# Delta-rule attention and an MLP on one core: w's product on two quarters of the array, copied out in one piece

## The chip, the cores and the metric

One core of a Trainium2 chip. The metric is the device time of one launch in microseconds (us). Engines: PE is TensorE (PEld its weight loads), ACT is ScalarE, DVE is VectorE, POOL is GpSimd, SP is SyncE, which issues most DMAs.

## The reference

For 4 batches and 8 heads, 768 steps and 48 dimensions a head, all float32, a state of 48x48 is carried along the steps by a delta rule; the attention's output, 3072 rows of 384, goes through an MLP with a squared ReLU.

```python
k_n = k / (np.linalg.norm(k, axis=-1, keepdims=True) + 1e-06)
for t in range(S):
    kt, vt, bt = (k_n[:, :, t], v[:, :, t], beta[:, :, t, None])
    y[:, :, t] = np.einsum('bhd,bhde->bhe', q[:, :, t], state)
    v_old = np.einsum('bhde,bhd->bhe', state, kt)
    state = state + bt[:, :, :, None] * np.einsum('bhd,bhe->bhde', kt, vt - v_old)
...
h = np.maximum(x @ w_in, 0.0)
return (h * h @ w_out).astype(np.float32)
```

## The kernel before, in words

**Units.** The 768 steps are cut into 12 units of 64 (C = 64). Inside a unit the recurrence is written as products of small matrices, so that a unit needs the state only at its start. For each unit and each of the 32 pairs of batch and head there is a 64x64 triangular matrix; its inverse, transposed and scaled, lies in `tt` (t in `state_part`). The unit's product w = t' v', where v' is v less what the state already holds for the keys (vt), gives the corrected values. From w come the state's update (keys' rows `kp` times w) and the unit's output y (masked query products `ap` times w, on top of queries times state). The MLP runs on a unit's 256 rows while the next unit's recurrence goes on.

**Layout.** 128 partitions are two halves of 64 (`half_rows(0)`, `half_rows(1)`). The index x (8 values) counts pairs of batch and heads, b (2) is a batch's place, j (2) a head's place and also picks one of two PSUM banks. The rows of a head (b, j) of t, vt, kp, ap and w lie in half b ^ j. A matmul of TensorE with 64 rows and 64 columns of weights takes one quarter of the array: the half of the partitions that it reads and the half of the PSUM partitions that it writes.

**The products of a unit**, all in `state_part` (line 720 on), 64 matmuls each (x by b by j):
- line 734: keys' rows times queries and state, two groups of four x; vt is corrected by VectorE (line 736), the query part is copied to `ap` by ScalarE (737) and masked by GpSimd.
- line 746: queries times state, into gy.
- line 752: w's product. In unit 0 (`first`) head (b, j) is read from half b ^ j and written to half b ^ j; in all other units it is read from half b ^ j and written to half b. So unit 0 uses two quarters, same half to same half, and the others all four.
- lines 759 to 764: ScalarE copies w from PSUM to SBUF. In unit 0 that is one copy (760). In the others the head j = 0 is in its place already (762), and for j = 1 each half of PSUM goes to the other half of SBUF (764, two copies of 64 partitions).
- line 774: the state's update, read from half b ^ j, written to the partitions of dims(j), four quarters, in all units but the last; VectorE adds it to the state (777).
- line 791: y's second part, read from half b ^ j, written to half b; ScalarE copies y (794).

Line 658 is unit 0's query products; it uses four quarters.

**Order.** The engines' queues keep the order in which the program is written. `weave` mixes the recurrence's generators with pieces of the MLP (`moe`: lines 845 and 829 are its matmuls, 852 to 855 ScalarE's squared ReLU and rounding, 820 VectorE's remainder, 805 to 808 the transposes of y and their split into x_h and x_l) by tables of fractions, A["odd"], A["even"] and A[u]. After w's product the queue of TensorE has MLP matmuls, then line 774. VectorE also works on the inverse of the next pair of units (lines 531 and 533) in small steps.

Of the kernel before, what the change touches and what calls it, by code (L numbers as in the profile page):

```python
# [20 lines left out]
def kernel(  # L21
# [89 lines left out]
    nc = tc.nc  # L111
# [23 lines left out]
    def g_tile():  # L135
        return ps_g.tile([P, 2, bank], F32, name="g")
# [56 lines left out]
    def need(*keys):  # L193
        assert all(key in done for key in keys), keys
# [126 lines left out]
    def half_rows(b):  # L321
        return slice(b * C, (b + 1) * C)

    def dims(j):
        return slice(j * C, j * C + D)
# [5 lines left out]
    def load_rows(dst, src, u):  # L331
        t = slice(u * C, (u + 1) * C)
        for b in range(2):
            for j in range(2):
                nc.sync.dma_start(out=dst[half_rows(b ^ j), j],
                                  in_=by_j(src)[j, 2 * b:2 * b + 2, :, t].rearrange("b p t d -> t (b p) d"))
# [307 lines left out]
    def masked(u):  # L644
        for b in range(2):
            half = ap[0][half_rows(b)].rearrange("p j x t -> p (j x) t")
            nc.gpsimd.affine_select(out=half, in_=half, pattern=[[0, 2 * X], [1, C]], base=0, channel_multiplier=-1,  # L647
                                    compare_op=ALU.is_gt, fill=0.0)
        done.add(("ap", u))
# [29 lines left out]
    def wide(g):  # L679
        return g[:, :, :XD].rearrange("p j (x e) -> p j x e", x=X)  # L680
# [4 lines left out]
    def turned_y(w, g):  # L685
        w_ = w.rearrange("p j x d -> p (j x d)")
        xt = g[:, :, :KT * 2 * C].rearrange("p b (k n t) -> p b k n t", k=KT, n=2)
        begun = set()

        def heads(j, p):  # L690
            for n in range(2):
                for part in range(2):
                    strip = 3 * p + part + j
                    kt, rows_ = strip // 4, slice(strip % 4 * HB, (strip % 4 + 1) * HB)
                    for r in range(2):
                        b = r ^ j
                        c0 = (j * X + n * NP + p) * C + (part * HB if j == 0 else part * HB - QB)
                        nc.tensor.matmul(xt[rows_, b, kt, n], lhsT=w_[half_rows(r), c0:c0 + HB],
                                         rhs=ap[0][half_rows(r), j, n * NP + p],
                                         start=(b, strip % 4) not in begun, stop=True, skip_group_check=True)  # L700
                        begun.add((b, strip % 4))
                yield

        for j in range(2):
            for ps in ((0, 2), (1, 3)):
                both = [heads(j, p) for p in ps]
                for n in range(2):
                    for gen in both:
                        next(gen)
            if j == 0:  # L710
                nc.tensor.drain()
        x_h, x_l = xs[0] = [mpool.tile([P, KT, 2 * P], F32R, name=name, bufs=1) for name in ("x_h", "x_l")]
        for k0, k1 in ((0, 1), (1, KT)):
            for b in range(2):
                cols = [x[:, k0:k1].rearrange("p k (n b t) -> p b (k n) t", n=2, b=2)[:, b] for x in (x_h, x_l)]
                src = xt[:, b, k0:k1].rearrange("p k n t -> p (k n) t")
                nc.scalar.copy(out=cols[0], in_=src)
                nc.vector.tensor_tensor(out=cols[1], in0=src, in1=cols[0].bitcast(F32), op=ALU.subtract)

    def state_part(u):  # L720
        first, last = u == 0, u == units - 1
        vt, t = vts[u], tt[:, :, u % 2].rearrange("p j x c t -> p j x (c t)")
        s = state.rearrange("p (b x) e -> p b x e", b=2)
        need(("v", u), ("keys", u), *[("y", u - 1)][:u])
        if not first:
            need(("queries", u))
            ap[0] = apool.tile([P, 2, X, C], F32, name="ap")
            for x0 in range(0, X, 4):
                ps = g_tile()[:, :, :4 * (C + D)].rearrange("p j (x n) -> p j x n", x=4)
                for x in range(4):  # L730
                    for b in range(2):
                        for j in range(2):
                            n = b * X + x0 + x
                            nc.tensor.matmul(ps[half_rows(b ^ j), j, x], lhsT=kts[u][dims(j), n], rhs=qs[dims(j), n],  # L734
                                             start=True, stop=True)
                nc.vector.tensor_tensor(out=vt[:, :, x0:x0 + 4], in0=vt[:, :, x0:x0 + 4], in1=ps[:, :, :, C:], op=ALU.subtract)  # L736
                nc.scalar.copy(out=ap[0][:, :, x0:x0 + 4], in_=ps[:, :, :, :C])  # L737
            masked(u)
            yield
        need(("queries", u), ("below", u))  # L740
        gy = g_tile() if first else wide(g_tile())
        if not first:
            for x in range(X):
                for b in range(2):
                    for j in range(2):
                        nc.tensor.matmul(gy[half_rows(b), j, x], lhsT=qts[u][dims(j), b * X + x], rhs=s[dims(j), b, x],  # L746
                                         start=x == 0, stop=False, skip_group_check=True)
        ps = wide(g_tile())
        for x in range(X):
            for b in range(2):  # L750
                for j in range(2):
                    nc.tensor.matmul(ps[half_rows(b ^ j if first else b), j, x], lhsT=t[half_rows(b ^ j), j, x],  # L752
                                     rhs=vt[half_rows(b ^ j), j, x],
                                     start=True, stop=True)
        if first:
            w = w0[0][:, :, :, :D]
        else:
            w = apool.tile([P, 2, X, D], F32, name="w")
        if first:
            nc.scalar.copy(out=w, in_=ps)  # L760
        else:
            nc.scalar.copy(out=w[:, 0], in_=ps[:, 0])
            for b in range(2):
                nc.scalar.copy(out=w[half_rows(1 - b), 1], in_=ps[half_rows(b), 1])
        done.add(("w", u))
        yield
        need(("ap", u), ("rows", u))
        def update():
            if not last:
                ps = wide(g_tile())  # L770
                for x in range(X):
                    for b in range(2):
                        for j in range(2):
                            nc.tensor.matmul(ps[dims(j), b, x], lhsT=kp[half_rows(b ^ j), j, x], rhs=w[half_rows(b ^ j), j, x],  # L774
                                             start=True, stop=True)
                for j in range(2):
                    nc.vector.tensor_tensor(out=s[dims(j)], in0=s[dims(j)], in1=ps[dims(j)], op=ALU.add)  # L777

        if first:
            turned_y(w0[0], gy)  # L780
            yield
            update()
            load_rows(kp, k, 1)
            done.update({("y", u), ("x", u)})
            yield
            return
        update()
        for x in range(X):
            for b in range(2):
                for j in range(2):  # L790
                    nc.tensor.matmul(gy[half_rows(b), j, x], lhsT=ap[0][half_rows(b ^ j), j, x], rhs=w[half_rows(b ^ j), j, x],  # L791
                                     start=False, stop=True, skip_group_check=True)
        ys[u] = y = apool.tile([P, 2, H * D], F32, name="y")
        nc.scalar.copy(out=y.rearrange("p n (q j e) -> p j (n q) e", j=2, e=D), in_=gy)  # L794
        done.add(("y", u))
        yield
# [167 lines left out]
    with tc.manual_schedule(engines=engines):  # L964
# [36 lines left out]
        def zeros():  # L1001
            need(("keys", 2), ("queries", 0))
            for b in range(2):
# [8 lines left out]
        chain = dict(A=kk[0], B=kk[1], P=prepare(pair0), I=inverse, G=query_products(0), V=scale_v(0, pair0),  # L1012
                     e=ended(pair0), c=corrected(pair0, 0), d=corrected(pair0, 1), b=below(pair0, 0), a=below(pair0, 1),
                     s=state_part(0))
        once = {"0": lambda: turned_keys(0, kb), "1": lambda: turned_keys(1, kb1), "2": lambda: turned_keys(2, kb3),
                "x": lambda: turned_queries(0, kb2), "y": lambda: turned_queries(1, kb), "l": later_loads,
# [81 lines left out]
```

## Time and profile before

| | us |
|---|---|
| median of 3 runs | 597.77 (596.33 to 599.57) |
| profiled execution, its own time | 595.15 |
| its span, first to last instruction | 593.4 |
| TensorE busy | 557.2 (94%) |
| VectorE busy | 395.2 (67%) |
| ScalarE busy | 334.4 (56%) |
| GpSimd busy | 53.9 (9%) |

The profiled execution is one more run, 2.6 us below the median of the others. A busy share is an average over stages; TensorE's is lower in the first 100 us (set-up, unit 0 and the splitting of the MLP's weights) than after. Weight loads and matmuls overlap, and so do matmuls among themselves, so a burst's busy time is the time from its first start to its last end less its gaps.

### The profile page before, as it was taken

To read this page: it belongs to the slowest core of one execution; us is meant where nothing else is said; L and a number is where in the kernel's file an instruction comes from. 1 tells how busy PE (TensorE), PEld (TensorE's weight loads), DVE (VectorE), ACT (ScalarE), POOL (GpSimd) and SP (SyncE) were. 2 spreads that over 40 slices of the span, in tenths; PEclk is the share of its full clock that TensorE was granted. 3 is DMA by queue.
4 is the path that set the end of the run, shared out by engine and by line. 5 is a ranking of instruction groups with operands and counts; after the bars stand their busy time and mean duration, and the time that the engine had idled before them with its cause. 6 is when DMAs were issued, how large, how long until landed. Compare 5 with 4: busy or idle time off the path is not lost.

```text
span 593.4 us, 21658 instructions
## 1 busy us (share of the span) xinstructions
PE 557.2 (94%) x9728; PEld 532.9 (90%) x9728; DVE 395.2 (67%) x725; ACT 334.4 (56%) x550; POOL 53.9 (9%) x64
## 2 busy tenths in 40 slices
PE   5276899989999999999999999999999999999997
PEld 5256799989899999999999999999999999999997
DVE  2899789899339798359798359797459795430210
ACT  4885578544756454665455566446565346564543
POOL 4020001101002002003002003002003002001000
PEclk9675689999999999999999999999999999999999
DMA  8967630140262050262050361140460330200101
GB/s 244 277 177 287 158 45 2 31 79 1 39 106 25 8 101 1 38 105 27 17 93 2 48 103 16 35 76 3 66 99 3 57 53 4 49 8 1 29 1 27
DMA packets 146668, 37.67 MB, mean 63 GB/s; under 512 B 140272, under 2 KB 143344, under 8 KB 146576
## 3 DMA queue, kind: packets, MB, share of 16 engines
q1 hardware_dynamic: 146496, 36.20, 29.9%
q8 instruction: 76, 1.25, 0.9%
q14 instruction: 16, 0.13, 0.1%
q10 hardware_dynamic: 80, 0.10, 0.0%
HBM read 31.56 MB, written 4.72 MB: 61 GB/s over the span
## 4 chain that ended last, share of the span: by engine, by line
PE 83%; ACT 7%; DVE 5%; DMA 2%; issue 1%; POOL 1%; SPq 1%; POOLq 0%; ACTq 0%
PE h L845 34%; PE o L829 30%; PE g L734 3%; PE g L829 2%; PE g L746 2%; PE g L791 2%; PE g L752 2%; PE g L774 1%; PE g L430 1%; PE g L392 1%; PE h L805 1%; ACT w L246 1%; DMA w<-in_moe_w_out_dram 1%; ACT w L248 1%; DVE w L278 1%
## 5 line engine op out<-in xcount | busy, mean ns | idle before, releaser
L829 PE MATMUL o<-w,h_h 128*128 128x384 f32 x704 | 185.7, 344 | 0.7 <-issue 0.7
L845 PE MATMUL h<-x_h,w 128*128 128x256 f32 x1152 | 173.4, 287 | 1.5 <-DVE x_l L808 1.5
L845 PEld LDWEIGHTS h<-x_h,w 128*128 128x128 f32 x1152 | 156.2, 193 | 4.9 <-issue 2.3
L820 DVE TENSOR_TENSOR h_l<-r,h_h 128x512 fp32r<-128x512 f32 x96 | 66.1, 692 | 125.3 <-ACT h_h L855 125.2
L829 PEld LDWEIGHTS o<-w,h_h 128*128 128x128 f32 x704 | 121.1, 189 | 3.9 <-issue 1.0
L829 PE MATMUL o<-w,h_l 128*128 128x384 f32 x352 | 118.2, 336 | 0.4 <-DVE h_l L820 0.4
L852 ACT ACTIVATE r<-h 128x512 f32<-128x512 f32 x96 | 57.5, 599 | 98.3 <-PE h L845 85.9
L845 PE MATMUL h<-x_l,w 128*128 128x256 f32 x576 | 101.1, 285 | 0.0
L845 PEld LDWEIGHTS h<-x_l,w 128*128 128x128 f32 x576 | 83.5, 193 | 0.0
L829 PEld LDWEIGHTS o<-w,h_l 128*128 128x128 f32 x352 | 66.0, 188 | 0.7 <-DVE h_l L820 0.7
L853 ACT ACTIVATE r<-r 128x512 f32<-128x512 f32 x96 | 60.7, 632 | 3.1
L855 ACT CAST h_h<-r 128x512 fp32r<-128x512 f32 x96 | 59.6, 621 | 3.0
L531 DVE TENSOR_TENSOR tmp<-lt,z 128x31 f32<-128x31 f32 (+15 forms) x155 | 56.4, 364 | 3.7
L533 DVE TENSOR_TENSOR z<-z,tmp 128x31 f32<-128x31 f32 (+15 forms) x155 | 53.1, 343 | 5.3
L647 POOL TENSOR_SCALAR_AFFINE_SELECT ap<-ap 64x1024 f32<-64x1024 f32 x24 | 33.0, 1376 | 245.0 <-ACT ap L737 241.5
L737 ACT COPY ap<-g 128x512 f32<-128x512 f32 x22 | 11.8, 590 | 35.3 <-DVE vt L736 35.3
L777 DVE TENSOR_TENSOR qs<-qs,g 48x768 f32<-48x768 f32 x22 | 20.9, 950 | 14.8 <-PE g L774 14.7
L794 ACT COPY y<-g 128x768 f32<-128x768 f32 x11 | 8.8, 801 | 27.8 <-PE g L791 27.7
L477 POOL MEMSET z<- 128x1024 f32 x5 | 4.8, 955 | 211.9 <-DVE lt L471 211.9
L807 ACT CAST x_h<-h 128x384 fp32r<-128x384 f32 x22 | 10.6, 481 | 23.2 <-PE h L805 23.2
L734 PE MATMUL g<-qs,kt 48*64 48x112 f32 x704 | 19.5, 259 | 0.2 <-DVE mt L449 0.2
L734 PEld LDWEIGHTS g<-qs,kt 48*64 48x64 f32 x704 | 17.1, 133 | 2.0 <-ACT mt L445 0.5
(165 smaller groups left out, 691.3 us busy)
## 6 DMA issues: line engine op xcount, KB each, us to landing
w<-in_moe_w_out_dram SPq DMA_DIRECT2D x8, 768.0 KB, 5.3
w<-in_moe_w_in_dram SPq DMA_DIRECT2D x6, 768.0 KB, 6.9
vt<-in_v_dram SPq DMA_DIRECT2D x48, 96.0 KB, 3.0
kp<-in_k_dram SPq DMA_DIRECT2D x48, 96.0 KB, 2.9
out_dram<-rest SPq DMA_DIRECT2D x47, 96.0 KB, 2.4
kb<-in_q_dram SPq DMA_DIRECT2D x40, 64.0 KB, 2.6
kb<-in_k_dram SPq DMA_DIRECT2D x32, 64.0 KB, 2.8
w<-in_moe_w_in_dram SPq DMA_DIRECT2D x3, 512.0 KB, 6.2
```

Of the source, the lines that this page charges most:

```text
L531: nc.vector.tensor_tensor(out=tmp, op=ALU.mult, in0=lt[:, s:s + 1, s + 1:].broadcast_to([P, nj, nt]), in1=z[:, :nj, s:s + 1].broadcast_to( ...
L533: nc.vector.tensor_tensor(out=z[:, :nj, s + 1:], in0=z[:, :nj, s + 1:], in1=tmp, op=ALU.subtract)
L647: nc.gpsimd.affine_select(out=half, in_=half, pattern=[[0, 2 * X], [1, C]], base=0, channel_multiplier=-1, compare_op=ALU.is_gt, fill=0.0)
L734: nc.tensor.matmul(ps[half_rows(b ^ j), j, x], lhsT=kts[u][dims(j), n], rhs=qs[dims(j), n], start=True, stop=True)
L746: nc.tensor.matmul(gy[half_rows(b), j, x], lhsT=qts[u][dims(j), b * X + x], rhs=s[dims(j), b, x], start=x == 0, stop=False, skip_group_che ...
L777: nc.vector.tensor_tensor(out=s[dims(j)], in0=s[dims(j)], in1=ps[dims(j)], op=ALU.add)
L820: nc.vector.tensor_tensor(out=h_l, in0=r, in1=h_h.bitcast(F32), op=ALU.subtract)
L829: nc.tensor.matmul(o[i], lhsT=a[:, e, i * P:(i + 1) * P], rhs=w_[w], start=(ft == 0 and n == 0), stop=(ft == FT - 1 and n == 2))
L845: nc.tensor.matmul(hp[:, e], lhsT=half_of(("wi", kt, part))[w][:, f], rhs=x[:, kt], start=(n == 0), stop=(n == 3 * KT - 1))
L852: nc.scalar.activation(out=r, in_=hp, func=AF.Relu)
L853: nc.scalar.activation(out=r, in_=r, func=AF.Square)
L855: nc.scalar.copy(out=h_h, in_=r)
```

## The change

In line 752 the output half becomes b ^ j in every unit, as it was in unit 0 alone, so that w lies in PSUM as it is wanted in SBUF; and ScalarE's copies become one copy of 128 partitions in every unit.

```diff
@@ -749,19 +749,14 @@
         for x in range(X):
             for b in range(2):
                 for j in range(2):
-                    nc.tensor.matmul(ps[half_rows(b ^ j if first else b), j, x], lhsT=t[half_rows(b ^ j), j, x],
+                    nc.tensor.matmul(ps[half_rows(b ^ j), j, x], lhsT=t[half_rows(b ^ j), j, x],
                                      rhs=vt[half_rows(b ^ j), j, x],
                                      start=True, stop=True)
         if first:
             w = w0[0][:, :, :, :D]
         else:
             w = apool.tile([P, 2, X, D], F32, name="w")
-        if first:
-            nc.scalar.copy(out=w, in_=ps)
-        else:
-            nc.scalar.copy(out=w[:, 0], in_=ps[:, 0])
-            for b in range(2):
-                nc.scalar.copy(out=w[half_rows(1 - b), 1], in_=ps[half_rows(b), 1])
+        nc.scalar.copy(out=w, in_=ps)
         done.add(("w", u))
         yield
         need(("ap", u), ("rows", u))
```

No other instruction is added, removed or moved on any engine. On ScalarE around w's copy of unit 1 (r and h_h are the MLP's, g a PSUM tile) the order before is:

```order
L852 ACTIVATE r<-h 128x512
L853 ACTIVATE r<-r 128x512
L855 CAST h_h<-r 128x512
L762 COPY w<-g 128x384
L764 COPY w<-g 64x384 x2
L852 ACTIVATE r<-h 128x512
```

and with the change, whose lines from 760 on have numbers smaller by 5:

```order
L847 ACTIVATE r<-h 128x512
L848 ACTIVATE r<-r 128x512
L850 CAST h_h<-r 128x512
L759 COPY w<-g 128x768
L847 ACTIVATE r<-h 128x512
```

The one copy stands where the three stood, in all of units 1 to 11.

## Rows read from the trace of the kernel before

**Rows 1.** The page, parts 1 and 2: busy time; granted clock in 40 slices, in tenths.

```profile
PE 557.2 (94%) x9728; PEld 532.9 (90%) x9728; DVE 395.2 (67%) x725; ACT 334.4 (56%) x550; POOL 53.9 (9%) x64
...
PEclk9675689999999999999999999999999999999999
```

**Rows 2.** The page, part 4: the chain that ended last, by engine.

```profile
PE 83%; ACT 7%; DVE 5%; DMA 2%; issue 1%; POOL 1%; SPq 1%; POOLq 0%; ACTq 0%
```

**Rows 3.** Stretches: from:to, length, each engine's busy time, granted clock, DMA.

```profile
194.00:545.00 351.00, 350.90 (x6086) 338.20 (x6085) 237.82 (x449) 190.79 (x316) 30.05 (x23) 1.00 0.26 43
...
150.00:194.00 44.00, 43.30 (x813) 41.53 (x813) 24.50 (x36) 27.27 (x45) 4.95 (x4) 1.00 0.36 56
```

**Rows 4.** TensorE's waits from 100 to 593 us: total, times, longest.

```profile
PE h L845 <- DVE x_l L808: 1.5, 1, 1.5
PE o L829 <- issue: 0.7, 1, 0.7
PE g L774 <- ACT w L764: 0.6, 1, 0.6
```

**Rows 5.** ScalarE's copies by line: shortest, median, longest in ns; first and last start.

```profile
L762 ACT COPY w<-g x11: 472/480/482, 110.8 to 544.2; 128x384 f32<-128x384 f32 x11
...
L764 ACT COPY w<-g x22: 471/474/478, 111.3 to 545.2; 64x384 f32<-64x384 f32 x22
...
L760 ACT COPY lt<-g x1: 799/799/799, 56.6 to 56.6; 128x768 f32<-128x768 f32 x1
```

**Rows 6.** Timeline of unit 8, TensorE and ScalarE: start, us, what.

```profile
420.65 0.48 ACT L762 COPY w<-g 128x384 f32<-128x384 f32 x1 [0.30 <-PE g L752]
421.15 0.96 ACT L764 COPY w<-g 64x384 f32<-64x384 f32 x2
...
422.83 0.94 PE L774 MATMUL g<-w,kp 64*48 64x48 f32 x64
```

**Rows 7.** w's products: matmuls and loads alone in stretches; durations in units 0, 1.

```profile
52.25:56.60 4.35, 4.03 (x64) 3.77 (x64) 0.50 1.03 413
...
53.30:55.86 2.56, 2.56 (x54) 2.56 (x52) 0.50 1.04 418
...
L752 PE MATMUL g<-vt,tt x60: 303/303/337, 52.3 to 55.9; 64*64 64x48 f32 x60
...
108.20:109.50 1.30, 1.11 (x64) 1.03 (x64) 1.00 0.06 13
...
108.50:109.10 0.60, 0.60 (x56) 0.60 (x49) 1.00 0.00 0
...
L752 PE MATMUL g<-vt,tt x64: 218/218/218, 108.3 to 109.2; 64*64 64x48 f32 x64
```

**Rows 8.** The same of line 658 (unit 0) and line 774 (units 0 and 7).

```profile
34.00:34.90 0.90, 0.90 (x47) 0.90 (x42) 0.50 0.44 132
...
L658 PE MATMUL g<-qs,kt x64: 311/311/366, 33.4 to 35.1; 48*64 48x64 f32 x64
...
60.35:61.11 0.76, 0.76 (x51) 0.76 (x47) 0.50 1.05 416
...
379.32:379.80 0.48, 0.48 (x60) 0.48 (x53) 1.00 0.00 0
...
L774 PE MATMUL g<-w,kp x640: 205/205/240, 112.3 to 510.4; 64*48 64x48 f32 x160
...
L774 PE MATMUL g<-lt,kp x64: 277/277/310, 60.0 to 61.3; 64*48 64x48 f32 x64
```

**Rows 9.** Timeline of unit 1: PE, PEld, ACT and DVE; idle time before in brackets.

```profile
110.85 0.47 ACT L762 COPY w<-g 128x384 f32<-128x384 f32 x1
...
112.34 0.81 PEld L774 LDWEIGHTS g<-w,kp 64*48 64x48 f32 x64 [0.83 <-ACT w L764]
...
122.17 1.02 DVE L808 TENSOR_TENSOR x_l<-h,x_h 128x384 fp32r<-128x384 f32 x2
...
122.87 0.95 PE L845 MATMUL h<-x_h,w 128*128 128x256 f32 x6 [1.48 <-DVE x_l L808]
```

## The prediction

> **What bounds the kernel now.** I read the page first. TensorE is busy for 94% of the span and its clock is granted at nine tenths or more from the seventh slice on [rows 1]; the reader is to see there that the lower digits end with the first sixth of the run, so that almost all units run at full clock. The chain that ended last is 83% TensorE, 7% ScalarE and 5% VectorE [rows 2]. A share over the whole span hides stages, so the third view is the table of stretches: from 194 to 545 us TensorE is busy 350.90 of 351.00 us, from 150 to 194 us 43.30 of 44.00, both at a granted clock of 1.00 [rows 3]. The bursts of w's products of units 3 to 11 lie in the long stretch, that of unit 2 in the one before, that of unit 1 at 108 us, a few us into the clock's last rise. In the long stretch nothing can be hidden beside TensorE: what its queue gains in work, the end gains in time. The fourth view, TensorE's waits after 100 us, confirms it: three entries, 2.8 us in all, and two of them belong to unit 1 (1.5 us for VectorE's x_l, 0.6 us for ScalarE's w); the third waits for no engine [rows 4].
>
> **What the change takes away.** In 11 units (1 to 11) three ScalarE copies of w, 480 ns and twice 474 ns, become one of 128x768. The same form is in the trace: unit 0's copy of w, which already goes in one piece, takes 799 ns [rows 5]. So 1.43 us becomes 0.80 us, 0.63 us a unit and 6.9 us of ScalarE over the run. On the path this is worth nothing in units 2 to 11: TensorE never waits for w there [rows 4]. Unit 8 shows how near it comes: the copies end at 421.15 + 0.96 = 422.11, and TensorE comes to the state's update, their reader, at 422.83 after MLP matmuls that it has anyway [rows 6]. The relief is credited at nothing in these units, since its cover is work that TensorE must do in any case.
>
> **What it adds.** The 64 matmuls of w's product (64x64 weights, 48 columns moving) in a unit are as many as before, in the same place of TensorE's queue. Before, they went over four quarters of the array: each half of the partitions read, into each half of PSUM. Now a half goes to the same half alone: two quarters. The question is what 64 such matmuls take on two quarters. The trace has it: unit 0 already runs this pattern, in the same form, but its stretch was granted 0.50 of the clock (the 1.2 GHz level), while the units after run at 1.00 (2.4 GHz) [rows 7]. So I take the rate at half clock and carry it over by bursts that ran at both.
>
> A window's count holds every matmul that runs in it, so N of them started within the window and one duration more. Unit 0, two quarters, half clock: 54 in 2.56 + 0.303 us, 53.0 ns each, 106 ns for two. Unit 1, four quarters, full clock: 56 in 0.60 + 0.218, 14.6 ns each, 58.4 ns for four [rows 7]. Two other bursts on four quarters bridge the two [rows 8]: the queries' products of unit 0 at half clock, 47 in 0.90 + 0.311, 25.8 ns each, 103 ns for four; and the state's update at both, in unit 0 51 in 0.76 + 0.277 (20.3 ns) and in unit 7 60 in 0.48 + 0.205 (11.4 ns). Two things follow. First, at half clock two matmuls on two quarters take as long (106 ns) as four on four (103 ns): each quarter takes its own next matmul after a time of its own, and half the quarters give half the rate. Second, full clock shortens that time by 20.3 / 11.4 = 1.78.
>
> So at full clock I expect two matmuls every 58.4 ns: 32 pairs instead of 16 fours, 16 x 58.4 = 0.93 us more for each unit (the burst busy 2.04 us instead of 1.11 [rows 7]). The ends: exactly half of 106 ns, 53.0 ns a pair, gives 32 x 53.0 - 16 x 58.4 = 0.76 us; 106 / 1.78 = 59.6 ns a pair gives 0.97 us; and unit 0's whole burst, 4.03 us (more than 64 x 53.0 ns and a duration, 3.7, so it also holds some stall), over 1.78 is 2.26 us, 1.15 us more than 1.11. I choose 0.93 because the same form at full clock is the nearest row.
>
> **Which units pay.** Units 2 to 11: TensorE is full around them, so all ten pay, 9.3 us. Unit 1 is special [rows 9]. There ScalarE is late: TensorE runs out of filler and waits 0.83 us (weights) until w is copied at 112.29. With the change the copy still starts at about 110.85, behind the cast that ends then, and ends at 111.65, while TensorE comes 0.93 us later: this wait goes and the update starts about 0.1 to 0.25 us later. Then TensorE waits again, 1.48 us, at 122.87 for x_l of the next MLP half, which VectorE begins at 122.17 without having waited for it (the row has no idle time before it): its own earlier work set that moment, and a delay of 0.25 us on TensorE vanishes in the 1.48. So unit 1 costs nothing, and also keeps nothing of the shorter copy. If that cover were gone it would pay its 0.93 - 0.83 = 0.1 us, at worst the whole 0.93.
>
> Nothing else goes late: w's copy starts 0.93 us later and ends 0.93 - 0.63 = 0.30 us later, but its reader also comes 0.93 us later, so the slack of 0.72 us in unit 8 (422.11 to 422.83) grows to 1.35. SyncE and GpSimd get nothing new. **Sum:** 10 x 0.93 = +9.3 us, no credit. Against the profiled execution (595.15 us, of which 593.4 span) that is 604.5 us. The three runs shown have a median of 597.77 (596.33 to 599.57); carried to it, 607.1 us, and that is what I forecast, +1.6%.
>
> **A rule that would give another sum.** The Trainium skill ("TensorE: Matmul & The Clock Gate", Part 3, The mechanism) says that a weight load runs beside matmuls in flight only where its row group differs. The order of the row halves (0, 1, 1, 0) is the same before and after; only the column half changes. By that rule alone the burst would last as long as now and the sum would be 0, which is rival (a) below. The trace disagrees with that reading: the state's update of unit 0 has the same order of row halves on four quarters and takes 20.3 ns a matmul at half clock, where unit 0's two quarters take 53.0 [rows 7, 8]; even with 64 weight columns for its 48 that would be 27.
>
> **The rivals.** *(a) The burst is no longer, and nothing is slower.* The place is the rate at full clock: if the order of the row halves sets it, which does not change, and what holds unit 0's burst back is the half clock or the traffic around it, 64 matmuls take 1.11 us again; the point at which this decides is a pair every 29 ns. Then nothing is added, unit 1 loses a wait of 0.83 us that the x_l wait takes back, and the time is 597.8, no change, 0.8 us less at most. For it: no burst on two quarters at full clock is in the trace. Against it: at half clock, the fours of unit 0 ran at twice the rate or more, the state's update beside the same DMA share (1.05 against 1.04) [rows 7, 8]. Chance 0.05. *(b) The clock falls in the burst.* Unit 0 shows the price of a stretch at 0.50: 4.03 us for the burst, 2.92 more than 1.11, over 10 units +29 us, 627 us. Against it: the clock is 1.00 from 150 to 545 us [rows 3], which holds ten units' bursts of small products, and the MLP's full-size matmuls stand on both sides. Chance 0.02. *(c) The burst is longer, but half of it finds a gap*, a time of about 602 or less. It needs idle time on TensorE, of which 0.10 us is left in 351 [rows 3]. Chance 0.03. That the change does not do what it says is hardly open: the order of instructions shows one copy of w a unit, and the quarter follows from the partitions. The forecast keeps 0.90.
>
> **How the numbers follow.** The bounds are 10 x 0.76 = 7.6 us and 11 x 1.15 = 12.7 us over 597.77, 605.4 to 610.5; the runs shown lie 1.4 below and 1.8 above their median, and the profiled execution 2.6 below it. I widen to 602.5 to 611.0. (b) and most of (a) lie outside. About 0.5% (3 us) is what a measurement of this kernel can tell from no change; the forecast, (b) and half of (c) are slower by more, (a) and the rest of (c) the same: slower 0.93, same 0.06, faster 0.01.
>
> **What would show it.** In the profile after: the burst of w's products busy about 2.04 us at full clock (1.9 to 2.3) in each of units 1 to 11, about 29 ns a matmul; one 128x768 copy of w of 0.80 us; no wait of TensorE for w in unit 1, with the x_l wait there shorter by a quarter of a microsecond or less; the update of the state in units 2 to 11 after the same filler; TensorE's busy time in the long stretch still whole. I am wrong if the burst keeps 1.1 us, if a stretch after 150 us has a granted clock below 1.00, or if TensorE gains idle time.

## The result and the profile after

The changed kernel takes 603.38 us (median of 4 runs, 601.18 to 605.48) against 597.05 us for the kernel before in the same comparison: ratio 1.0127, 95% interval 1.0096 to 1.0157, which is 5.7 to 9.4 us more. It is slower, as forecast; the forecast time was 607.1. Compared again with more runs of the kernel before (first experiment below) the ratio was 1.0165 (1.0124 to 1.0206).

One correction to the words ahead of the prediction: x by b by j is 32 products, not 64. The trace shows each of these float32 products as two matmuls and two weight loads; the 64 are what the trace counts, and all rates are for these.

The page of the changed kernel, parts 1, 2 and 4, whose lines answer to [rows 1, 2]; its line numbers from 760 on are smaller by 5 (the state's update is line 769, the MLP's 840 and 824):

```profile
span 600.9 us, 21634 instructions
...
PE 561.7 (93%) x9728; PEld 538.4 (90%) x9728; DVE 395.5 (66%) x725; ACT 327.3 (54%) x528; POOL 53.9 (9%) x64
...
PEclk9675899999999999999999999999999999999999
...
PE 87%; ACT 4%; DVE 4%; DMA 2%; issue 2%; SPq 1%; DVEq 0%; ACTq 0%
```

ScalarE is busy 7.1 us less, where 11 x 0.63 = 6.9 was said, and TensorE 4.5 us more; that is only half of the 9.3 forecast because TensorE was busy 5.3 us less in the set-up, of which more below (the fifth and sixth slices show a higher clock than before). The chain is TensorE's even more than it was.

Stretches of the changed kernel (columns as in [rows 3]):

```profile
150.00:194.00 44.00, 43.50 (x811) 41.99 (x810) 24.38 (x37) 25.38 (x41) 5.13 (x4) 1.00 0.34 54
194.00:552.00 358.00, 357.92 (x6077) 345.40 (x6077) 237.45 (x447) 185.34 (x299) 29.87 (x22) 1.00 0.25 42
```

TensorE is as full as before, and the clock is whole. w's products in units 1 and 7, of line 752 alone, which answer to [rows 7], and ScalarE's copies, which answer to [rows 5]:

```profile
106.90:109.30 2.40, 2.05 (x64) 1.96 (x64) 1.00 0.03 7
...
374.20:376.60 2.40, 2.05 (x64) 1.96 (x64) 1.00 0.00 0
...
L752 PE MATMUL g<-vt,tt x64: 218/218/218, 107.0 to 108.8; 64*64 64x48 f32 x64
...
L759 ACT COPY w<-g x11: 795/802/804, 109.6 to 551.7; 128x768 f32<-128x768 f32 x11
```

The burst is busy 2.05 us instead of 1.11 at full clock; one matmul still lasts 218 ns. Only fewer run at once. (What the 58.4 ns between two matmuls on one quarter consist of, no run here takes apart.) The copy takes 802 ns.

Timeline of unit 8 of the changed kernel, which answers to [rows 6]:

```profile
423.28 2.07 PE L752 MATMUL g<-vt,tt 64*64 64x48 f32 x64
...
425.40 0.80 ACT L759 COPY w<-g 128x768 f32<-128x768 f32 x1 [1.32 <-PE g L752]
...
427.56 0.81 PEld L769 LDWEIGHTS g<-w,kp 64*48 64x48 f32 x64 [0.25 <-issue]
```

w is there at 426.20, 1.36 us before its reader. And unit 1, which answers to [rows 9]:

```profile
109.06 0.62 ACT L850 CAST h_h<-r 128x512 fp32r<-128x512 f32 x1
109.59 0.80 ACT L759 COPY w<-g 128x768 f32<-128x768 f32 x1
...
111.30 0.81 PEld L769 LDWEIGHTS g<-w,kp 64*48 64x48 f32 x64
...
120.92 1.02 DVE L803 TENSOR_TENSOR x_l<-h,x_h 128x384 fp32r<-128x384 f32 x2
...
121.62 0.95 PE L840 MATMUL h<-x_h,w 128*128 128x256 f32 x6 [1.28 <-DVE x_l L803]
```

No wait for w is left; the wait for x_l is 1.28 us instead of 1.48.

Where the time came in is seen by one and the same instruction in both traces: the start of the state's update (line 774 before, 769 after), read from the two timelines, with some starts of line 734 between (differences of unrounded times).

```
                     before    after   after less before
line 734, unit 1      96.81    95.55   -1.27
update, unit 1       112.35   111.30   -1.04
line 734, unit 2     140.07   138.82   -1.25
update, unit 2       159.77   160.13   +0.36
line 734, unit 3     184.81   184.17   -0.64
update, unit 3       204.75   205.04   +0.30
update, unit 4       248.78   249.73   +0.95
update, unit 5       291.91   293.80   +1.88
update, unit 6       335.97   338.76   +2.80
update, unit 7       379.10   382.83   +3.73
update, unit 8       422.83   427.56   +4.73
update, unit 9       465.97   471.63   +5.66
update, unit 10      509.67   516.27   +6.60
line 791, unit 11    550.59   558.11   +7.53
```

Units 2 to 11 together add 8.8 us (from -1.25 to +7.53). From unit 5 on every unit adds 0.91 to 1.00 us, unit 3 adds 0.93 and unit 4 0.65; unit 1 adds 0.02. Unit 2 adds 1.6 and then takes 1.0 back, mostly since each trace has a pause of TensorE there that the other has not, before (first line) and after:

```profile
163.24 0.19 PEld L829 LDWEIGHTS o<-w,h_h 128*128 128x128 f32 x1 [1.02 <-issue]
...
155.12 0.73 PEld L746 LDWEIGHTS g<-qs 48*64 48x64 f32 x43 [0.57 <-issue]
```

Ahead of unit 1 the profiled execution of the changed kernel was 1.27 us faster. The change touches nothing there; what the trace shows to differ is the granted clock, though that it makes up all of the 1.27 us is not shown. The stretch up to line 734, the one from there to the end, and the one from 61.5 to 78.6 us, before:

```profile
0.00:96.81 96.81, 67.26 (x1660) 59.85 (x1661) 77.00 (x130) 67.58 (x107) 11.78 (x32) 0.75 0.66 182
...
96.81:593.40 496.59, 489.91 (x8068) 473.02 (x8068) 318.24 (x596) 266.85 (x444) 42.17 (x32) 1.00 0.24 40
...
61.50:78.60 17.10, 14.28 (x420) 13.19 (x417) 14.00 (x22) 8.70 (x15) 0.00 (x0) 0.60 0.55 102
```

and after:

```profile
0.00:95.55 95.55, 61.98 (x1661) 55.06 (x1661) 77.03 (x130) 67.37 (x107) 11.78 (x32) 0.80 0.66 185
...
95.55:600.90 505.35, 499.75 (x8068) 483.34 (x8068) 318.47 (x596) 259.92 (x422) 42.15 (x32) 1.00 0.24 40
...
61.50:78.60 17.10, 12.40 (x505) 11.02 (x497) 14.86 (x24) 9.37 (x16) 0.00 (x0) 0.90 0.55 108
```

In the set-up the same work (1660 and 1661 matmuls) ran at a granted clock of 0.75 on average in one and 0.80 in the other; between 61.5 and 78.6 us it was 0.60 and 0.90. TensorE was busy 5.3 us less there, and 9.8 us more from line 734 on, for the same 8068 matmuls: 4.5 in all.

### The profile page after: what moved, and what is told of

Its sections match the earlier page's. It is cut to its first block, busy times and chain, and to the rows that moved or that the text cites. A ratio compares the mean times of both kernels' runs of the same rounds, so it can differ in the third digit from the quotient of the medians.

```text
span 600.9 us, 21634 instructions
## 1 busy us (share of the span) xinstructions
PE 561.7 (93%) x9728; PEld 538.4 (90%) x9728; DVE 395.5 (66%) x725; ACT 327.3 (54%) x528; POOL 53.9 (9%) x64
## 3 DMA queue, kind: packets, MB, share of 16 engines
q8 instruction: 76, 1.25, 0.8%
## 4 chain that ended last, share of the span: by engine, by line
PE 87%; ACT 4%; DVE 4%; DMA 2%; issue 2%; SPq 1%; DVEq 0%; ACTq 0%
PE h L840 34%; PE o L824 30%; PE g L752 3%; PE g L734 3%; PE g L824 2%; PE g L746 2%; PE g L786 2%; PE g L769 1%; PE g L430 1%; PE g L392 1%; PE h L800 1%; DMA ap<-in_k_dram 1%; DVE a L290 1%; DVE w L278 1%; ACT w L246 1%
## 5 line engine op out<-in xcount | busy, mean ns | idle before, releaser
L840 PEld LDWEIGHTS h<-x_h,w 128*128 128x128 f32 x1152 | 154.6, 191 | 5.9 <-issue 3.5
L752 PE MATMUL g<-vt,tt 64*64 64x48 f32 x768 | 26.8, 225 | 1.0 <-issue 1.0
L752 PEld LDWEIGHTS g<-vt,tt 64*64 64x64 f32 x768 | 25.6, 141 | 1.2 <-issue 1.2
```

The source lines that it names most:

```text
L752: nc.tensor.matmul(ps[half_rows(b ^ j), j, x], lhsT=t[half_rows(b ^ j), j, x], rhs=vt[half_rows(b ^ j), j, x], start=True, stop=True)
L840: nc.tensor.matmul(hp[:, e], lhsT=half_of(("wi", kt, part))[w][:, f], rhs=x[:, kt], start=(n == 0), stop=(n == 3 * KT - 1))
```

## The experiments

The theory: what counts is how many quarters of the array are in use, and the cost is on TensorE alone. "Two quarters" and "four quarters" are as in the prediction. Since the set-up differs from execution to execution, the table gives for each profile the span less the start of unit 1's line 734 (the steady part). `row_half`, `column_half`, `runs_of_two` and `one_quarter` ran in one execution each (602.04, 601.64, 595.65 and 623.56 us, beside 597.68 for one of the kernel before). The three other kernels with four quarters in units 1 to 11 lie within 0.4 us of the kernel before in the steady part.

```
                       span    line 734   steady part   against before
before                593.4      96.8        496.6
changed kernel        600.9      95.5        505.4         +8.8
pairs_again           601.4      95.3        506.1         +9.5
pairs_three_copies    602.5      97.2        505.3         +8.7
row_half              600.3      94.7        505.6         +9.0
column_half           599.9      94.3        505.6         +9.0
fours_one_copy        592.9      96.6        496.3         -0.3
runs_of_two           593.9      96.9        497.0         +0.4
fours_in_unit0        598.7     101.8        496.9         +0.3
one_quarter           621.8      95.4        526.4        +29.8
```

**The changed kernel once more** (no edit).

> The changed kernel once more. Theory (half the quarters, half the rate; 0.93 us a unit in units 2 to 11, unit 1 free): from the first burst of line 734 (start of the steady part) to the end of the span about 9 us longer than in the kernel before (496.6 us), whatever the set-up before it took, and a time 8 to 9.5 us over the kernel before. Rival (part of the burst is absorbed somewhere, and the true cost is the 6.3 us that the two medians showed): 6 to 7 us over, and the steady part no more than 7 us longer.

Measured: ratio 1.0165 (1.0124 to 1.0206), 603.6 us against 595.32, which is the median of 23 runs of the kernel before. By the ratio that is 9.8 us more (7.4 to 12.3); the medians are 8.3 us apart. The steady part is 9.5 us longer. The rival of 6.3 us falls: the changed kernel's median is the same in both comparisons (603.38 and 603.6), and the first one's base, 4 runs from 593.74 to 599.57, was at the high side.

**Four quarters, one copy.**

```diff
-        if first:
-            nc.scalar.copy(out=w, in_=ps)
-        else:
-            nc.scalar.copy(out=w[:, 0], in_=ps[:, 0])
-            for b in range(2):
-                nc.scalar.copy(out=w[half_rows(1 - b), 1], in_=ps[half_rows(b), 1])
+        nc.scalar.copy(out=w, in_=ps)
```

> The matmuls of the kernel before, on four quarters, with the one copy of the change: w's halves for j = 1 are left exchanged, so the numbers are not the reference's, but the work is the same. Theory: the copies are off the path; the burst stays 1.11 us, the wait of 0.83 us for w in unit 1 goes but comes back as a longer wait for x_l; time 0 to 0.8 us below the kernel before, not to be told from it. Rival (the copies are on the path and the change's relief pays back part of its cost): 2 to 6 us faster.

Measured: ratio 1.0010 (0.9985 to 1.0036). The relief of ScalarE alone is worth nothing that can be measured. In unit 1 (timeline, then TensorE's waits after 100 us) the wait for w shrinks from 0.83 to 0.16 us and comes back as a wait for x_l of 1.9 us instead of 1.5:

```profile
110.63 0.79 ACT L759 COPY w<-g 128x768 f32<-128x768 f32 x1
111.47 0.81 PEld L769 LDWEIGHTS g<-w,kp 64*48 64x48 f32 x64 [0.16 <-ACT w L759]
```

```profile
PE h L840 <- DVE x_l L803: 1.9, 1, 1.9
```

**Two quarters, three copies.**

```diff
-                    nc.tensor.matmul(ps[half_rows(b ^ j if first else b), j, x], lhsT=t[half_rows(b ^ j), j, x],
+                    nc.tensor.matmul(ps[half_rows(b ^ j), j, x], lhsT=t[half_rows(b ^ j), j, x],
...
-                nc.scalar.copy(out=w[half_rows(1 - b), 1], in_=ps[half_rows(b), 1])
+                nc.scalar.copy(out=w[half_rows(b), 1], in_=ps[half_rows(b), 1])
```

> The matmuls of the change, on two quarters, with three copies as before (each half to the same half). Theory: all of the cost is in the matmuls; time as the changed kernel's within 1 us, some 9 us over the kernel before; in unit 1 TensorE comes to the update at about the same moment as w (within 0.4 us). Rival (the shorter copy pays back part): 2 to 6 us slower than the changed kernel.

Measured: ratio 1.0135 (1.0108 to 1.0163), steady part +8.7 us: the whole cost without the relief. In unit 1 w is ready at 112.50 and the update starts 0.42 us later, at 112.92, without a wait:

```profile
111.54 0.96 ACT L764 COPY w<-g 64x384 f32<-64x384 f32 x2
...
112.92 0.81 PEld L774 LDWEIGHTS g<-w,kp 64*48 64x48 f32 x64
```

The two parts of the change thus add up: matmuls about +9 us, copies 0.

**Two quarters of one row half.** Edit on top of four quarters with one copy:

```diff
-                    nc.tensor.matmul(ps[half_rows(b ^ j if first else b), j, x], lhsT=t[half_rows(b ^ j), j, x],
-                                     rhs=vt[half_rows(b ^ j), j, x],
+                    nc.tensor.matmul(ps[half_rows(b ^ j if first else b), j, x], lhsT=t[half_rows(b ^ j if first else 0), j, x],
+                                     rhs=vt[half_rows(b ^ j if first else 0), j, x],
```

> Two quarters again, but two that share a half of the rows: in units 1 to 11 all of w's products read half 0 and write to half b (so w is that of other heads; one copy; the outputs are not the reference's). The order of the row halves is 0, 0, 0, 0 instead of 0, 1, 1, 0. Theory (the rate is set by how many quarters are in use): burst busy 2.0 to 2.1 us, as in the changed kernel. Rival (weight loads run beside matmuls in flight only where the row half differs, so the order of the row halves sets the rate): the burst is longer than the changed kernel's, 3 us or more.

The burst in unit 5:

```profile
284.50:286.90 2.40, 2.07 (x64) 1.98 (x64) 1.00 0.03 7
```

**Two quarters of one column half.**

```diff
-                    nc.tensor.matmul(ps[half_rows(b ^ j if first else b), j, x], lhsT=t[half_rows(b ^ j), j, x],
-                                     rhs=vt[half_rows(b ^ j), j, x],
+                    nc.tensor.matmul(ps[half_rows(b ^ j if first else 0), j, x], lhsT=t[half_rows(b ^ j if first else j), j, x],
+                                     rhs=vt[half_rows(b ^ j if first else j), j, x],
...
-            nc.scalar.copy(out=w[:, 0], in_=ps[:, 0])
             for b in range(2):
-                nc.scalar.copy(out=w[half_rows(1 - b), 1], in_=ps[half_rows(b), 1])
+                nc.scalar.copy(out=w[half_rows(b)], in_=ps[half_rows(0)])
```

> Two quarters that share a half of the columns: head (b, j) is read from half j and written to half 0 of PSUM bank j, in the order of row halves 0, 1, 0, 1; two copies of 64 partitions bring that half to both halves of w (the outputs are not the reference's). Theory (number of quarters): burst busy 2.0 to 2.1 us. Rival (the order of the row halves sets the rate): 1.1 us, as on four quarters. A second rival (the columns' side is the bound): over 3 us.

The burst in unit 5:

```profile
284.50:286.90 2.40, 2.03 (x64) 1.95 (x64) 1.00 0.03 7
```

Three ways to choose two quarters out of four (same half to same half, one row half, one column half) give 2.05, 2.07 and 2.03 us. The rule of the Trainium skill that the prediction weighed ("TensorE: Matmul & The Clock Gate", Part 3, The mechanism: a weight load runs beside matmuls in flight only where the row group differs) would make the row-half run slower than the column-half run; the expectations put that at 3 us or more against 1.1. Here the two are 0.04 us apart.

**Four quarters, runs of two.**

```diff
-        for x in range(X):
-            for b in range(2):
-                for j in range(2):
+        for b, j, x in [(b, j, x) for x0 in range(0, X, 2) for b in range(2) for j in range(2) for x in (x0, x0 + 1)]:
```

> The kernel before, with four quarters and the same results, but two values of x follow each other on a quarter before the next quarter's turn (A A B B C C D D instead of A B C D). Theory in its weak form (each quarter has work queued of its own, so only the number of quarters counts): burst 1.1 us and no change. In its strong form (matmuls start in the order of the queue, and one that waits for its quarter holds back those behind it): each run of two costs a second turn, burst 1.6 to 2.1 us, as if two quarters were in use.

The burst in unit 7:

```profile
371.50:373.00 1.50, 1.22 (x64) 1.13 (x64) 1.00 0.00 0
```

1.22 us instead of 1.11: neither 1.1 nor 1.6. The steady part is 0.4 us longer, which one execution cannot tell from none. The strong form fails for runs this short (two products, four of the trace's matmuls, on a quarter before the next one's turn).

**One quarter at a time.** Edit on top of the changed kernel:

```diff
+        order = [(x, b, j) for x in range(X) for b in range(2) for j in range(2)]
+        for x, b, j in order if first else sorted(order, key=lambda n: n[1] ^ n[2]):
```

> The changed kernel with its order changed in units 1 to 11: first all products of half 0, then all of half 1, so that one quarter works at a time; one copy, same results. Theory in the strong form (matmuls start in the order of the queue): 64 turns of 58.4 ns, burst 3.7 to 3.9 us, 1.9 us more than the changed kernel in each unit and some 18 us in all (10 units or 11), 621 us. Weak form (each quarter draws its own work from the queue, however far back): burst 2.0 us as in the changed kernel, same time.

Its bursts in units 5 and 7, of line 751 alone (w's product there):

```profile
293.10:297.10 4.00, 3.70 (x64) 3.62 (x64) 1.00 0.02 4
385.10:389.10 4.00, 3.70 (x64) 3.62 (x64) 1.00 0.00 0
```

The steady part is 29.8 us longer than before, 21.0 more than the changed kernel's, where some 18 were expected; the clock, below, is part of the difference. In the burst, first start to last start is 3.70 - 0.22 = 3.48 us, where 64 turns of 58.4 ns one after the other would be 63 x 58.4 = 3.68: about three or four turns of the second half overlap the first. So for long runs the strong form holds: work for a free quarter is not drawn from far back in the queue. Together with the runs of two: a few turns are.

In two of the units (4 and 11) the shift against the kernel before grew by 4.1 us instead of the 2.3 to 2.8 (mostly 2.6) of units 5 to 10. There the clock fell. Around unit 4's burst, which starts at 250.18 (columns of [rows 3]):

```profile
250.10:253.70 3.60, 3.60 (x87) 3.60 (x77) 0.69 (x1) 0.61 (x1) 0.00 (x0) 0.99 0.18 19
253.70:257.10 3.40, 3.40 (x14) 3.31 (x12) 0.00 (x0) 0.80 (x1) 0.00 (x0) 0.50 0.02 5
257.10:260.00 2.90, 2.90 (x135) 2.59 (x134) 1.27 (x2) 0.43 (x1) 0.00 (x0) 1.00 0.00 0
```

TensorE is busy throughout, but as a burst on one quarter ends its clock is granted at 0.50, and then at 1.00 again. The page's clock row of this kernel shows it in three places (units 1, 4 and 11):

```profile
PEclk9995799899999999899999999999999999998999
```

This is the prediction's rival (b), at a price of about 1.5 us in units 4 and 11, where (b) had put it at 2.9 a unit. None of the five profiles with two quarters has it.

**Four quarters in unit 0 as well.**

```diff
-                    nc.tensor.matmul(ps[half_rows(b ^ j if first else b), j, x], lhsT=t[half_rows(b ^ j), j, x],
+                    nc.tensor.matmul(ps[half_rows(b), j, x], lhsT=t[half_rows(b ^ j), j, x],
...
-        if first:
-            nc.scalar.copy(out=w, in_=ps)
-        else:
-            nc.scalar.copy(out=w[:, 0], in_=ps[:, 0])
-            for b in range(2):
-                nc.scalar.copy(out=w[half_rows(1 - b), 1], in_=ps[half_rows(b), 1])
+        nc.scalar.copy(out=w[:, 0], in_=ps[:, 0])
+        for b in range(2):
+            nc.scalar.copy(out=w[half_rows(1 - b), 1], in_=ps[half_rows(b), 1])
```

> The other way round: unit 0's products also go over four quarters, with three copies, everything else as before. Theory: at half clock a quarter takes its next matmul after 106 ns, whether two or four are in use; unit 0's burst falls from 3.93 us (first to last start) to about 1.7 to 2.2 us, if the clock there is the same; w's copy gets 0.63 us longer and is waited for there, so unit 0 gains 1.1 to 1.6 us and the kernel at most that, perhaps nothing, as VectorE or the weights' splitting may set the pace there. Rival (it was the half clock or the DMA traffic that made unit 0's burst slow): the burst stays above 3.4 us and the time is that of the kernel before or 0.6 us longer.

Unit 0's burst, whole and its last part, and its copies (columns of [rows 3], then of [rows 6]):

```profile
54.20:58.00 3.80, 2.62 (x64) 2.25 (x64) 0.50 1.03 414
56.75:57.53 0.78, 0.78 (x30) 0.78 (x29) 0.50 1.04 420
...
56.73 1.10 PE L752 MATMUL g<-vt,tt 64*64 64x48 f32 x30 [0.78 <-issue]
...
57.88 0.48 ACT L759 COPY lt<-g 128x384 f32<-128x384 f32 x1 [0.65 <-PE g L752]
58.38 0.96 ACT L761 COPY lt<-g 64x384 f32<-64x384 f32 x2
```

Behind an idle stretch of 0.78 us that no engine's work ends, 30 matmuls start within about 0.8 us, 27 ns each where two quarters take 53 at the same clock and the same DMA share: so it was the quarters, not the clock or the traffic. The rate is as expected, the burst is not: with that stretch inside it, it takes 3.29 us from first to last start, less than 3.93 but far from 1.7 to 2.2. What is gained, 0.64 us, the copies take back: one of 0.80 us becomes three, 1.46 us from first start to last end, and from the burst's first start to w's last copy both kernels need 5.1 us. So the time is that of the kernel before: ratio 1.0012 (0.9988 to 1.0035). The set-up of this one profile is 5.0 us longer than before's; from 46 to 84 us its granted clock was 0.51 where before's was 0.62, and 1.9 of the 5.0 us had come in before the burst starts, so it says nothing of the edit.

## Why the prediction was right, step by step

- **TensorE bounds units 2 to 11.** Right: the long stretch stays full (357.92 of 358.00), and units 5 to 11 each shift all that follows by 0.91 to 1.00 us. One reading beside it was wrong: unit 1's burst at 108 us is not a few us behind the clock's last rise but 30; from 78.7 us on the clock of the kernel before is 1.00. Nothing hangs on it.
- **Half the quarters, half the rate; 16 x 58.4 ns = 0.93 us.** Right to a hundredth: 2.05 us measured, 2.04 forecast. The step from half clock to full clock held, and the two other pairs of quarters gave the same. The reason given with it (each quarter has its own next matmul) needs a limit that the prediction did not have: it holds for products that are close together in the queue, as the run with one quarter at a time shows.
- **The copies bring nothing.** Right: one copy alone 1.0010, three copies with two quarters 1.0135.
- **Unit 1 is free.** Right: the update there 0.23 us later against its own start (-1.04 after -1.27), taken back before unit 2.
- **The sum.** Right: 9.3 us were forecast; the five profiles with two quarters have a steady part 8.7 to 9.5 us longer, 9.0 on average, all against the one profile of the kernel before. In the pair shown above what is missing lies in units 2 and 4, which add 0.6 us each. In unit 2 most of it is idle time of TensorE that the profile assigns to "issue" and that falls differently from one profile to the next: the 0.7 us of [rows 4] ahead of line 829 is not in the changed kernel's waits, one of 0.5 us ahead of line 746 is. In unit 4 the cause stays open.
- **The time.** 607.1 was 3.7 us high, and 603.38 lies below the bounds that the sum itself gave (605.4 to 610.5); it is inside the forecast's range because that was widened downwards for the scatter of the runs. The step that was off is the base: "carried to it" meant the median of three runs, 597.77, where 23 runs have 595.32; 595.32 + 9.3 = 604.6 is 1.0 to 1.2 us from the two medians measured, and so is the 604.5 that the prediction had from the profiled execution and passed over. The profile's own time moves by microseconds with the set-up: line 734 of unit 1 starts between 94.3 and 101.8 us.
- **Rival (a)** fell with the burst itself. **Rival (b)** did not happen here, but did on one quarter. **Rival (c)**, half of the cost lost in a gap, is what 6.3 us in the first comparison looks like; it falls with the steady parts, none of which is less than 8.7 us longer.

## What to carry to other kernels

Here 64 matmuls (as the trace counts them) of 64x64 weights and 48 columns in float32 took 1.11 us on four quarters of the array, 2.03 to 2.07 on two, in three choices of the two, and 3.70 on one: the rate was set by how many quarters took part. Products for different quarters must stand close together in the queue. Other shapes were not run on two quarters or on one. A layout that saves another engine's copies by using fewer quarters pays in TensorE's time; by the same sum it is worth it only where that engine, and not TensorE, ends last. And if executions differ by a stage that the change does not touch, compare from an instruction behind that stage on.

## What the runs showed of the hardware that was not expected

A burst of small products on one quarter, 3.70 us long and without a gap, was in three of eleven units followed by a stretch of 3.4 us at half clock that began within 0.4 us of its end, while TensorE was busy throughout; bursts of 2.05 us on two quarters never were. And work that stands a whole half-burst ahead of its turn in the queue is not drawn forward to a free quarter: of 32 matmuls for the idle quarter, three or four overlapped.
